# Two row tiles that share each weight chunk, and the exponentials of A's keys one product later

## The chip, the cores and the metric

The kernel runs on one core of a Trainium2 chip. A core has a matrix engine (TensorE, "PE" in the profile), a vector engine (VectorE, DVE), a scalar engine (ScalarE, ACT), GpSimd (POOL) and a queue processor that only issues transfers (SyncE, SP). They run side by side, each through its own list of instructions in order, and wait for each other on semaphores. Matrix products write into PSUM; the other operands lie in SBUF; inputs and outputs lie in HBM and are moved by 16 DMA engines.

The metric is the device time of one execution, in microseconds (us). The kernel before takes 461.2 us, the median of seven runs between 460.77 and 463.86.

## What is computed

x has 2048 rows of 1024 numbers. Two attention blocks read it and a gate per row mixes them:

```python
g = sigmoid((x * gate_w).sum(-1))
a = A(x)          # linear attention: phi(t) = where(t > 0, t + 1, exp(t)) + 1e-6
b = B(x)          # local attention: 8 keys behind each row, 2 apart, softmax
out = g * a + (1 - g) * b
# A: q, k, v = x @ A_wqkv, in 32 heads of 32
#    kv = sum over rows of phi(k)^T v,  z = sum over rows of phi(k)
#    o  = (phi(q) kv) / (phi(q) z),     a = o @ A_wo
# B: q, k, v = x @ B_wqkv, in 32 heads of 32
#    b = (softmax(q k / sqrt(32)) v) @ B_wo
```

The change touches two places: the very first product, x times the v columns of B_wqkv, and the phi of A's keys.

## The kernel before

**Tiles.** The rows of x are taken in 16 tiles of 128. A *pair* is two of them; tile_of(pair, i) names them, so that pair 0 is tiles 0 and 4, pair 1 tiles 1 and 5, pair 2 tiles 2 and 6. xT holds x transposed: the 1024 columns lie as 8 chunks of 128 partitions, so that a product of a tile with 512 columns of weights is eight matmuls (kc 0 to 7) into one PSUM tile. Most products are done as groups with seven products in place of eight, on sums of operands that VectorE makes (class Group, m1 to m7; Weights.sums and xsums make the sums); the sequence of these products is the clock of the program: side() is called after each of them.

**The start.** Before any sum can be there, pairs 0 and 1 are multiplied plainly with the v weights of B (vb_plain, called in L880). The weights arrive in 256 KB pieces: vb_load(k, j) brings the chunks kc = 2k and 2k + 1 of column half j. Piece (0, 0) is issued by ScalarE's queue, all others by SP's. Two tiles, 0 and 4, come as plain rows (xr_load, L189) and are transposed by TensorE (transpose, L469): eight 128x128 transposes into two PSUM tiles, the first half copied to xT by ScalarE, the second by VectorE (L478). All other tiles are transposed by the DMA on the way in (xt_load, L90). SP issues in this order (L191 to L203): rows of tile 0; pieces (1, 0), (2, 0), (3, 0); rows of tile 4; tiles 1 and 5 transposed; the four pieces of half 1; tiles 2, 6, 3 and 7 transposed.

vb_plain first goes through column half 0 tile by tile: tile 0, 4, 1, 5, each with its eight matmuls (L520), then the gate's eight narrow matmuls (gate, L456) and ScalarE's copy out of PSUM (v_final, L244). The transposes of tile 0 stand before kc 0 of tile 0, those of tile 4 before kc 6 of tile 0. Then half 1 is done for all four tiles chunk by chunk. Fourteen matmuls on zeros (warm_up, L467) stand ahead of all this.

**Who sets the order.** TensorE's and SP's lists are as the program writes them (manual_schedule, L40). The lists of the other engines are ordered by a scheduler that keeps to the order of emission, save where high_priority() or issue_after() say otherwise.

**The keys of A.** ka_group multiplies a pair with A's key columns. When the last column half of a tile is in SBUF (tA), done(i) takes a tile eA and calls phi (L543): phi emits the exponential on ScalarE at once, and returns three VectorE steps (maximum, minimum, sum). defer(n, ops) queues such steps; side() adds one to the count of products, state["now"], then calls dve_side(), which emits the next step of the first queue whose time has come, and only then step(), which emits pieces of side work such as the scores of B's attention with their large exponential (PT, L701). qa_group also calls phi, for some of A's queries, and emits all its steps at once.

Of the kernel before, what the change touches and what calls it, by code (L numbers as in the profile page):

```python
# [8 lines left out]
ACT = mybir.ActivationFunctionType  # L9
ALU = mybir.AluOpType  # L10
# [16 lines left out]
def kernel(  # L27
# [11 lines left out]
    nc = tc.nc  # L39
# [13 lines left out]
    def xrows(t):  # L53
        return xpar[t // 8, (t % 8) * P:(t % 8 + 1) * P, :]
# [128 lines left out]
    def vb_load(k, j, q=nc.sync):  # L183
        q.dma_start(out=W[:, 2 * k:2 * k + 2, 512 * j:512 * j + 512],
                    in_=bview[:, 2 * k:2 * k + 2, 2 * D + 512 * j:2 * D + 512 * j + 512])
# [3 lines left out]
    def xr_load(t):  # L189
        xr[t] = ering.tile([P, D], BF16, name="xr", tag="e")  # L190
        nc.sync.dma_start(out=xr[t][:], in_=xrows(t))  # L191
    vb_load(0, 0, nc.scalar)
    xr_load(0)
    vb_load(1, 0)
    vb_load(2, 0)
    vb_load(3, 0)
    xr_load(4)
    for t in (1, 5):
        xt_load(t)
    for k in range(4):  # L200
# [41 lines left out]
    def acc(out_, ps, add):  # L242
        if add is None:
            nc.scalar.copy(out=out_, in_=ps)  # L244
        else:
            last_dve[0] = nc.vector.tensor_tensor(out=out_, in0=ps, in1=add, op=ALU.add).ins
# [3 lines left out]
    class Group:  # L250
# [10 lines left out]
        def mm(self, ps, m, start):  # L261
            for kc in range(self.nk):
                lhsT, rhs = self.operands(m, kc)
                nc.tensor.matmul(ps[:], lhsT=lhsT, rhs=rhs, start=start and kc == 0,  # L264
                                 stop=kc == self.nk - 1, skip_group_check=True)
# [68 lines left out]
    def row_ops(w, pair):  # L334
        p, c = divmod(pair, 4)
        return lambda m, kc: (xop(m, kc, p, slice(c * P, c * P + P)), w.get(m, kc))
# [58 lines left out]
    def defer(products, ops, gap=1):  # L395


        deferred.append([state["now"] + products, list(ops), gap])
# [46 lines left out]
    def tile_of(pair, i):  # L445
        return (pair // 4) * 8 + (pair % 4) + 4 * i
# [5 lines left out]
    def gate(t):  # L452
        p, j = divmod(t, 8)
        hf, c = divmod(j, 4)
        for kc in range(8):
            nc.tensor.matmul(gps[:, t:t + 1], lhsT=xT[p][:, kc, hf, c * P:(c + 1) * P], rhs=gw[:, kc:kc + 1],  # L456
                             start=kc == 0, stop=kc == 7)
# [11 lines left out]
    def transpose(t):  # L469
        p, j = divmod(t, 8)  # L470
        hf, c = divmod(j, 4)
        for k0, tag, copy in ((0, "X1", nc.scalar.copy), (4, "Y1", nc.vector.tensor_copy)):
            tps = ps_pj.tile([P, 512], F32, name="tps", tag=tag)
            tps = tps.bitcast(BF16)[:, 0:512].rearrange("p (k n) -> p k n", k=4)
            for k in range(4):
                nc.tensor.transpose(tps[:, k, :], xr[t][:, (k0 + k) * P:(k0 + k + 1) * P], ident[:])
            with tc.high_priority():
                last_dve[0] = copy(out=xT[p][:, k0:k0 + 4, hf, c * P:(c + 1) * P], in_=tps).ins  # L478


    def v_tiles(name):
        if name == "va":
            return [tring.tile([P, H, 32], BF16, name=name, tag="t") for _ in range(2)]
        vs = [tring.tile([P, H, 33], BF16, name=name, tag="t") for _ in range(2)]
        for v in vs:
            nc.gpsimd.memset(v[:, :, 32:33], 1.0)  # L486
        return vs

    def v_final(vs, by_chunk=False):
        def final(i, j, ps, add):  # L490
            if by_chunk:
                out_ = vs[i][:].rearrange("p (c a h) e -> p a c h e", c=4, a=2)[:, j, :, :, 0:32]
                rs = lambda ap: ap.rearrange("p (c h e) -> p c h e", c=4, e=32)
            else:
                out_ = vs[i][:, 16 * j:16 * j + 16, 0:32]
                rs = lambda ap: ap.rearrange("p (h e) -> p h e", e=32)
            acc(out_, rs(ps), None if add is None else rs(add))
        return final

    def vb_store(vs, pair, i):  # L500
        t = tile_of(pair, i)
        nc.sync.dma_start(out=V_d[t // 8][(t % 8) * P:(t % 8 + 1) * P, :],
                          in_=vs[i][:].rearrange("p h e -> p (h e)"))
# [5 lines left out]
    def vb_plain(*pairs):  # L509


        vs = {pair: v_tiles("va") for pair in pairs}
        tiles = [(pair, i) for pair in pairs for i in range(2)]

        def ps_of(pair, i):
            return ps_pj.tile([P, 512], F32, name="K", tag="XY"[i] + str(pair % 2))

        def mm(ps, pair, i, j, kc):
            p, c = divmod(pair, 4)
            nc.tensor.matmul(ps[:], lhsT=xT[p][:, kc, i, c * P:c * P + P],  # L520
                             rhs=wvB.W[:, kc, 512 * j:512 * j + 512], start=kc == 0, stop=kc == 7,
                             skip_group_check=True)
        for pair, i in tiles:
            ps = ps_of(pair, i)
            for kc in range(8):
                if (pair, i) == tiles[0] and kc in (0, 6):
                    transpose(tile_of(pair, kc // 6))
                mm(ps, pair, i, 0, kc)
            gate(tile_of(pair, i))
            v_final(vs[pair], True)(i, 0, ps[:], None)  # L530
        tiles = tiles[2:] + tiles[:2]
        ps = {t: ps_of(*t) for t in tiles}
        for k in range(4):
            for t in tiles:
                for kc in (2 * k, 2 * k + 1):
                    mm(ps[t], *t, 1, kc)
                if k == 3:
                    pair, i = t
                    v_final(vs[pair], True)(i, 1, ps[t][:], None)
                    vb_store(vs[pair], pair, i)  # L540


    def phi(e, t):  # L543

        nc.scalar.activation(out=e, in_=t, func=ACT.Exp)  # L545
        return [lambda: nc.vector.tensor_scalar(out=t, in0=t, scalar1=0.0, scalar2=None, op0=ALU.max),
                lambda: nc.vector.tensor_scalar(out=e, in0=e, scalar1=1.0, scalar2=EPS, op0=ALU.min, op1=ALU.add),
                lambda: nc.vector.tensor_tensor(out=e, in0=e, in1=t, op=ALU.add)]  # L548

# [3 lines left out]
    def ka_group(w, pair):  # L553
        ts = [tring.tile([P, D], BF16, name="tA", tag="t") for _ in range(2)]

        def final(i, j, ps, add):
            acc(ts[i][:, 512 * j:512 * j + 512], ps, add)

        def done(i):
            e = ering.tile([P, D], BF16, name="eA", tag="e")  # L560
            defer(0, phi(e[:], ts[i][:]))
            pks[tile_of(pair, i)] = e
        return Group(row_ops(w, pair), final, done)

# [70 lines left out]
    def qa_group(w, nn, p):  # L635
        ts = [tring.tile([P, 2, 512], BF16, name="tq", tag="t") for _ in range(2)]
        es = [ering.tile([P, 2, 512], BF16, name="eq", tag="e") for _ in range(2)]
        out = qa_out(es, nn, p)

        def final(i, j, ps, add):  # L640
            acc(ts[i][:, j, :], ps, add)

        def done(i):
            for f in phi(es[i][:], ts[i][:]):
                f()
            add_side(8, out(i), p, "oa")
        return Group(col_ops(w, p), final, done)
# [228 lines left out]
    def gates(*pairs):  # L876
        for pair in pairs:
            for i in range(2):
                gate(tile_of(pair, i))
    vb_plain(0, 1)  # L880
    x_loads(4, 5)
    ws, xs = wvB.sums(), xsums(2)
# [117 lines left out]
```

## Time and profile before

| what | us |
|---|---|
| median of seven runs | 461.2 |
| the profiled execution | 460.77 |
| its span, first to last instruction | 459.0 |
| TensorE busy | 443.2 |
| VectorE busy | 283.1 |
| ScalarE busy | 236.9 |
| GpSimd busy | 59.7 |
| 16 exponentials eA of 1024 columns, each | 1.06 |
| 16 large exponentials PT, each | 1.87 |
| 512-column matmul L520, mean of one in the records | 0.38 |

The page is one execution. A record of a matmul is longer than its slot, since matmuls are pipelined: in a run of them the starts stand 0.22 us apart. Where the page says "x<-y", x is written and y is read; "<-DMA xr" behind a row in brackets says for whom the engine stood idle, and how long. The 40 digits of the page's second part are slices of 11.5 us each:

```profile
PE   7999999998999999999999999999999999999996
...
DMA  9799911690301703007030056291229772795111
```

The reader is to see that in the first slice TensorE is busy to seven tenths only, while the DMA engines are nearly full.

### The profile page before, as it was taken

To read this page: it belongs to the slowest core of one execution; us is meant where nothing else is said; L and a number is where in the kernel's file an instruction comes from. 1 tells how busy PE (TensorE), PEld (TensorE's weight loads), DVE (VectorE), ACT (ScalarE), POOL (GpSimd) and SP (SyncE) were. 2 spreads that over 40 slices of the span, in tenths; PEclk is the share of its full clock that TensorE was granted. 3 is DMA by queue.
4 is the path that set the end of the run, shared out by engine and by line. 5 is a ranking of instruction groups with operands and counts; after the bars stand their busy time and mean duration, and the time that the engine had idled before them with its cause. 6 is when DMAs were issued, how large, how long until landed. Compare 5 with 4: busy or idle time off the path is not lost.

```text
span 459.0 us, 11712 instructions
## 1 busy us (share of the span) xinstructions
PE 443.2 (97%) x5017; PEld 216.4 (47%) x5070; DVE 283.1 (62%) x452; ACT 236.9 (52%) x345; POOL 59.7 (13%) x119
## 2 busy tenths in 40 slices
PE   7999999998999999999999999999999999999996
PEld 4455444444444444444445444445554444444444
DVE  0456768669748387485774846769777973256112
ACT  2234357567476484673855847536677544222221
POOL 8000000000000000000000000007686313000000
PEclk9999999999999999999999999999999999999999
DMA  9799911690301703007030056291229772795111
GB/s 213 155 231 225 306 26 70 200 197 3 99 4 36 157 1 101 1 26 164 6 99 2 26 131 193 90 263 47 71 72 222 169 169 91 148 212 134 48 46 46
DMA packets 111956, 51.62 MB, mean 112 GB/s; under 512 B 75552, under 2 KB 107552, under 8 KB 111904
## 3 DMA queue, kind: packets, MB, share of 16 engines
q1 hardware_dynamic: 111600, 50.61, 45.5%
q8 instruction: 39, 0.64, 0.6%
q10 hardware_dynamic: 272, 0.26, 0.2%
q14 instruction: 13, 0.11, 0.1%
q0 software_dynamic: 32, 0.00, 0.0%
HBM read 26.22 MB, written 16.78 MB: 94 GB/s over the span
## 4 chain that ended last, share of the span: by engine, by line
PE 89%; ACT 6%; DMA 1%; issue 1%; DVE 0%; SPq 0%; ACTq 0%; DVEq 0%
PE X L264 41%; PE Y L264 28%; PE Q L661 9%; PE K L520 3%; ACT PT L701 3%; PE o L712 2%; PE oA L618 2%; ACT eA L545 2%; PE s L696 1%; DMA xr<-in_A_x_dram 1%; PE kps L579 1%; ACT tA L244 1%; PE o L717 1%; PE Y L299 1%; ACT U2s L273 1%
## 5 line engine op out<-in xcount | busy, mean ns | idle before, releaser
L264 PEld LDWEIGHTS <-xT 128*128 128x128 bf16 (+1 forms) x352 | 33.0, 98 | 39.7 <-issue 1.8
L264 PE MATMUL X<-T,SS 128*128 128x512 f16 x176 | 45.3, 380 | 0.7 <-ACT U2s L273 0.7
L264 PEld LDWEIGHTS <-WS 128*128 128x128 bf16 (+1 forms) x288 | 28.1, 98 | 33.6
L661 PE MATMUL Q<-xT,WS 128*128 128x512 bf16 x186 | 43.1, 379 | 0.3
L264 PE MATMUL X<-SS,TS 128*128 128x512 f16 x144 | 37.0, 379 | 3.9 <-ACT U2s L273 3.9
L273 ACT COPY U4s<-X 128x512 f32<-128x512 f32 x40 | 23.4, 584 | 33.0 <-PE X L264 32.9
L486 POOL MEMSET vA<- 128x32 bf16 x16 | 4.0, 250 | 269.6 <-DVE eA L548 144.8
L264 PE MATMUL Y<-W,xT 128*128 128x512 bf16 (+1 forms) x151 | 38.8, 379 | 0.0
L264 PEld LDWEIGHTS <-SS 128*128 128x128 f16 x264 | 24.2, 98 | 29.7 <-issue 2.8
L701 ACT ACTIVATE PT<-s 128x2048 bf16<-128x2048 f32 x16 | 29.9, 1869 | 15.1 <-PE s L696 15.0
L264 PE MATMUL Y<-xT,WS 128*128 128x512 bf16 (+1 forms) x144 | 36.9, 379 | 0.0
L264 PEld LDWEIGHTS <-TS 128*128 128x128 f16 x216 | 20.4, 97 | 29.0 <-issue 5.9
L702 DVE TENSOR_TENSOR PT<-PT,maskp 128x2048 bf16<-128x2048 bf16 x16 | 19.6, 1224 | 22.1 <-ACT PT L701 22.1
L273 ACT COPY M1s<-X 128x512 f32<-128x512 f32 x40 | 23.6, 589 | 11.5 <-PE X L264 10.4
L661 PEld LDWEIGHTS <-WS 128*128 128x128 bf16 x192 | 18.3, 98 | 20.1
L273 ACT COPY U2s<-X 128x512 f32<-128x512 f32 x40 | 23.3, 583 | 8.2 <-PE X L264 8.2
L264 PEld LDWEIGHTS <-oT 128*128 128x128 bf16 (+1 forms) x176 | 17.2, 98 | 20.5
L629 POOL TENSOR_TENSOR obA<-ofv,rec 128x512 bf16<-128x512 f32 x22 | 25.7, 1187 | 0.9
L724 DVE COPY nB<-o 128x1024 f32<-128x1024 f32 x16 | 19.6, 1222 | 6.0 <-ACT rB L723 6.0
L723 ACT ACTIVATE rB<-o 128x1024 f32<-128x1024 f32 x16 | 16.4, 1023 | 12.3 <-DVE oB L730 9.5
L264 PE MATMUL X<-T,oS 128*128 128x512 f16 x96 | 22.7, 379 | 0.0
L264 PE MATMUL X<-W,SS 128*128 128x512 bf16 x86 | 22.5, 379 | 0.1
(140 smaller groups left out, 760.2 us busy)
## 6 DMA issues: line engine op xcount, KB each, us to landing
V_d<-va SPq DMA_DIRECT2D x16, 256.0 KB, 3.2
WS<-in_B_wqkv_dram SPq DMA_DIRECT2D x16, 256.0 KB, 4.5
W<-in_A_wqkv_dram SPq DMA_DIRECT2D x8, 512.0 KB, 6.2
vw<-V_d SPq DMA_DIRECT2D x16, 256.0 KB, 4.3
OB_d<-oB SPq DMA_DIRECT2D x16, 256.0 KB, 2.2
OA_d<-obA SPq DMA_DIRECT2D x16, 256.0 KB, 2.3
out_dram<-osb SPq DMA_DIRECT2D x30, 128.0 KB, 1.8
oT<-OB_d SPq DMA_DIRECT2D x12, 256.0 KB, 4.0
```

The source lines that it names most:

```text
L264: nc.tensor.matmul(ps[:], lhsT=lhsT, rhs=rhs, start=start and kc == 0, stop=kc == self.nk - 1, skip_group_check=True)
L273: nc.scalar.copy(out=s[:], in_=ps[:])
L520: nc.tensor.matmul(ps[:], lhsT=xT[p][:, kc, i, c * P:c * P + P], rhs=wvB.W[:, kc, 512 * j:512 * j + 512], start=kc == 0, stop=kc == 7, ski ...
L545: nc.scalar.activation(out=e, in_=t, func=ACT.Exp)
L618: nc.tensor.matmul(o[:, k, 132 * j:132 * j + 132], lhsT=es[i][:, j, k * P:(k + 1) * P], rhs=KVz[:, nn + 4 * j, :], start=True, stop=True)
L629: nc.gpsimd.tensor_tensor(out=ob[:, k:k + 2], in0=of[:, k:k + 2, :, 0:32], in1=rec[:, k:k + 2].broadcast_to([P, 2, 8, 32]), op=ALU.mult)
L661: nc.tensor.matmul(ps[:], lhsT=w.W[:, kc, j * P:j * P + P], rhs=xT[p][:, kc, i, :], start=kc == 0, stop=kc == 7, skip_group_check=True)
L701: nc.scalar.activation(out=PT[:], in_=s[:], func=ACT.Exp, scale=SCALE)
L702: nc.vector.tensor_tensor(out=PT[:], in0=PT[:], in1=maskp[:, None, :].broadcast_to([P, 4, 512]), op=ALU.mult)
L712: nc.tensor.matmul(o[32 * g:32 * g + 32, 2 * b, cols], lhsT=vw[rows, j, 4 * ch + g, :], rhs=PT[rows, g, cols], start=True, stop=True)
L723: nc.scalar.activation(out=rB[:], in_=o[:, 1:4:2, :], func=ACT.Ln)
L724: nc.vector.tensor_copy(out=nB[:], in_=o[:, 0:4:2, :])
```

## The change

There are three edits.

- SP issues the rows of tile 4 directly behind the rows of tile 0, ahead of the three weight pieces.
- vb_plain takes tiles 0 and 4 through half 0 together, two chunks at a time: kc 0 and 1 of tile 0, then of tile 4, then kc 2 and 3 of tile 0, and so on. The transposes of each stand before its own kc 0. Their gates and copies out of PSUM follow behind both. Tiles 1 and 5 are done as before.
- phi no longer emits the exponential itself: the exponential becomes part of its first deferred step, together with the maximum. ka_group defers by 1 in place of 0. qa_group calls all steps at once, as before.

```diff
--- before.py
+++ after.py
@@ -191,10 +191,10 @@
         nc.sync.dma_start(out=xr[t][:], in_=xrows(t))
     vb_load(0, 0, nc.scalar)
     xr_load(0)
+    xr_load(4)
     vb_load(1, 0)
     vb_load(2, 0)
     vb_load(3, 0)
-    xr_load(4)
     for t in (1, 5):
         xt_load(t)
     for k in range(4):
@@ -520,14 +520,20 @@
             nc.tensor.matmul(ps[:], lhsT=xT[p][:, kc, i, c * P:c * P + P],
                              rhs=wvB.W[:, kc, 512 * j:512 * j + 512], start=kc == 0, stop=kc == 7,
                              skip_group_check=True)
-        for pair, i in tiles:
-            ps = ps_of(pair, i)
-            for kc in range(8):
-                if (pair, i) == tiles[0] and kc in (0, 6):
-                    transpose(tile_of(pair, kc // 6))
-                mm(ps, pair, i, 0, kc)
-            gate(tile_of(pair, i))
-            v_final(vs[pair], True)(i, 0, ps[:], None)
+        ps = {t: ps_of(*t) for t in tiles[:2]}
+        for k in range(4):
+            for t in tiles[:2]:
+                if k == 0:
+                    transpose(tile_of(*t))
+                for kc in (2 * k, 2 * k + 1):
+                    mm(ps[t], *t, 0, kc)
+        for t in tiles:
+            if t not in ps:
+                ps[t] = ps_of(*t)
+                for kc in range(8):
+                    mm(ps[t], *t, 0, kc)
+            gate(tile_of(*t))
+            v_final(vs[t[0]], True)(t[1], 0, ps[t][:], None)
         tiles = tiles[2:] + tiles[:2]
         ps = {t: ps_of(*t) for t in tiles}
         for k in range(4):
@@ -542,8 +548,8 @@
 
     def phi(e, t):
 
-        nc.scalar.activation(out=e, in_=t, func=ACT.Exp)
-        return [lambda: nc.vector.tensor_scalar(out=t, in0=t, scalar1=0.0, scalar2=None, op0=ALU.max),
+        return [lambda: (nc.scalar.activation(out=e, in_=t, func=ACT.Exp),
+                         nc.vector.tensor_scalar(out=t, in0=t, scalar1=0.0, scalar2=None, op0=ALU.max)),
                 lambda: nc.vector.tensor_scalar(out=e, in0=e, scalar1=1.0, scalar2=EPS, op0=ALU.min, op1=ALU.add),
                 lambda: nc.vector.tensor_tensor(out=e, in0=e, in1=t, op=ALU.add)]
 
@@ -558,7 +564,7 @@
 
         def done(i):
             e = ering.tile([P, D], BF16, name="eA", tag="e")
-            defer(0, phi(e[:], ts[i][:]))
+            defer(1, phi(e[:], ts[i][:]))
             pks[tile_of(pair, i)] = e
         return Group(row_ops(w, pair), final, done)
```

## The prediction

> **What bounds the kernel now.** I read the page's busy times first, then the chain of waits over the first 60 us, then the timeline from 0 to 40 us and the landing times of single DMA issues, and last the order of the instructions of both built programs on each engine. The busy times say that TensorE sets the time: no other engine is near it.
>
> ```profile
> PE 443.2 (97%) x5017; PEld 216.4 (47%) x5070; DVE 283.1 (62%) x452; ACT 236.9 (52%) x345; POOL 59.7 (13%) x119
> ```
>
> So only a place where TensorE stands still, or an instruction taken from it, can move the end. The change takes no TensorE instruction away. The chain of waits (start, length, what) shows one long step that isn't TensorE's, right at the start:
>
> ```profile
> 2.67 6.24 DMA xr<-in_A_x_dram
> 8.96 0.62 PE tps L476 x8
> 9.58 0.43 PE K L520 x2
> ...
> 11.94 0.18 PE gps L456 x8
> 12.12 1.75 PE K L520 x8
> ```
>
> The second row load is issued at 2.67, lands 6.24 later, and only then can TensorE transpose tile 4. A whole product of a tile costs 1.75, or 0.216 for one of eight matmuls, and a gate 0.18. The timeline of the same stretch (start, length, engine, line, what):
>
> ```profile
> 0.74 0.39 SPq L191 DMA_DIRECT2D xr<-in_A_x_dram  x1
> 1.20 1.43 SPq L184 DMA_DIRECT2D W<-in_B_wqkv_dram  x3
> 2.67 0.47 SPq L191 DMA_DIRECT2D xr<-in_A_x_dram  x1
> ...
> 4.52 1.04 PE L476 MATMUL tps<-ident,xr 128*128 128x128 bf16 x8 [0.16 <-POOL maskp L217]
> 5.17 0.58 ACT L478 COPY xT<-tps 128x512 bf16<-128x512 bf16 x1 [3.15 <-PE tps L476]
> 5.81 1.89 PE L520 MATMUL K<-W,xT 128*128 128x512 bf16 x6 [0.25 <-ACT xT L478]
> ...
> 8.96 0.62 PE L476 MATMUL tps<-ident,xr 128*128 128x128 bf16 x8 [1.26 <-DMA xr<-in_A_x_dram]
> ...
> 9.39 0.58 ACT L478 COPY xT<-tps 128x512 bf16<-128x512 bf16 x1 [3.64 <-PE tps L476]
> ...
> 11.98 1.89 PE L520 MATMUL K<-W,xT 128*128 128x512 bf16 x8
> ```
>
> The reader is to see three things. TensorE idles 1.26 (1.42 by issue slots: the sixth matmul starts at 7.32 and needs 0.22) before the second eight transposes. The first product of tile 1 starts at 11.98; everything up to there belongs to tiles 0 and 4. And all five loads before 3.19 stand in one line on SP's queue.
>
> **The change, part one: the start.** SP's issue of the tile 4 rows moves ahead of three weight loads. Landings, each issue's start plus its latency in the trace: first rows 0.74 + 3.7 = 4.5; chunk 0 (ACT's queue) 0.77 + 4.4 = 5.2; chunks 1, 2, 3 at 1.20 + 4.7 = 5.9, 1.66 + 5.4 = 7.1, 2.16 + 6.1 = 8.2; tile 4 rows 2.67 + 6.2 = 8.9. Consecutive landings are 0.7 to 1.2 apart and all six loads are 256 KB, so I treat the landings as slots in order of issue. Tile 4's rows then take the slot at 5.9 (no later than 7.1, if the fabric serves them one slot late); chunks 1, 2, 3 land at 7.1, 8.2 and 8.9. The sum of bytes is unchanged, so the transposing loads of tiles 1 and 5 behind them, which land at 3.19 + 6.6 = 9.8 and 5.03 + 6.3 = 11.3, stay there.
>
> TensorE's new order, from the same start 5.81: two matmuls of tile 0, at 5.81 and 6.21; their weight loads stand 0.4 apart and the third comes at 6.53. The eight transposes of tile 4 therefore begin at 6.53, with their rows there since 5.9. The first half of the tile is copied by ScalarE: in the trace that copy starts 0.43 after the transposes (9.39 against 8.96), takes 0.58, and a matmul follows 0.05 behind the copy in the first tile (5.17 + 0.58 to 5.81). So tile 4's first matmul starts at 6.53 + 0.43 + 0.58 + 0.06 = 7.60. Transposes end near 7.0, so TensorE now idles about 0.6 for the copy, which before was hidden behind tile 0's last two matmuls and its gate. Then 14 matmuls follow: 14 x 0.216 = 3.02, to 10.62. Chunks are needed at 7.60 + 0.43 = 8.03, 8.89 and 9.76, against landings at 7.1, 8.2 and 8.9: 0.7 to 0.9 to spare each. Two gates at 0.2 each (9.85 to 10.05 in the trace) bring tile 1's first product to **11.03 instead of 11.98: 0.95 less**. Its columns landed at 9.8; tile 5 is needed at 12.96 and landed at 11.3. With the rows a slot late (7.1) the same sum gives 11.6, a gain of 0.4; with no wait for the copy at all it would be 1.55, which nothing here allows.
>
> What is late next? The second halves of the weights land by 14.8 and are first used at 14.9. VectorE's sums for pair 2 hang on a transposing load, not on TensorE:
>
> ```profile
> 18.26 0.42 DVE L100 TENSOR_TENSOR SS<-xT 128x512 f16<-128x512 bf16 x1 [4.13 <-DMA xT<-in_A_x_dram]
> ...
> 22.35 0.42 DVE L102 TENSOR_TENSOR SS<-xT,SS 128x512 f16<-128x512 bf16 x1
> ...
> 23.42 0.43 DVE L103 TENSOR_TENSOR xT<-xT 128x512 f16<-128x512 bf16 x1 [0.65 <-PE gps L456]
> ...
> 26.33 1.03 PE L264 MATMUL Y<-T3v,xT 128*128 128x512 f16 x4
> ```
>
> These sums stay at 18.26 to 22.77; the last one (L103) waits for TensorE's gates and moves up to 22.77, ending at 23.2, while its matmul comes at 25.4 instead of 26.33. There are 2.2 to spare. From the V_d stores at 22.45 on, SP's loads follow TensorE's results, with DMA idle from 20 to 22, so they move up too. I find nothing tied to absolute time behind that, and let the 0.95 run through to the end.
>
> **A rule against it.** "TensorE: Matmul & The Clock Gate", section "HAM oscillation — how this bites in real kernels", says to run all chunks of one tile before waiting for DMA, since an idle window of about 3.4 us drops the clock to half; the change does the opposite. Taken by its letter, 14 matmuls at the 0.4 of the first two cost 14 x 0.2 = 2.8 more, and the sum is 1.9 slower. The row: after 1.26 idle before tile 4's transposes the eight took 0.62 against 1.04 for tile 0's, and the matmuls behind them stand 0.216 apart. (The granted clock reads 1.00 in both stretches; only the spacing shows the slow beginning.) The longest stretch without products is 6.53 to 7.60 in the new order, shorter than the old 7.54 to 9.42, so I take the row.
>
> **Part two: the exponentials.** They matter for TensorE where one stands before a large exponential on ScalarE:
>
> ```profile
> 104.02 1.06 ACT L545 ACTIVATE eA<-tA 128x1024 bf16<-128x1024 bf16 x1
> ...
> 104.99 1.86 ACT L701 ACTIVATE PT<-s 128x2048 bf16<-128x2048 f32 x1
> ...
> 106.74 0.58 ACT L273 COPY U2s<-X 128x512 f32<-128x512 f32 x1
> ...
> 107.37 0.81 PE L264 MATMUL X<-SS,TS 128*128 128x512 f16 x3 [0.61 <-ACT U2s L273]
> ```
>
> The view of waits has 4.5 us of this kind in 7 stalls. But the edit can't reach them: side() raises the product count before it looks at deferred work, so an entry of delay 1 comes out in the same call as one of delay 0, and dve_side() runs ahead of the step() that emits the large exponential. The built programs agree: on ScalarE, VectorE and GpSimd the order is the same throughout, and every wait after the start is on the same count; TensorE differs in its first 160 instructions alone, SP in four issues. Cost and gain: nothing.
>
> **Sum.** Span 459.0 - 0.95 = 458.05; the profiled execution took 460.77, 1.77 more than its span, so 459.8. The median of the seven runs is 461.2: **460.3**.
>
> **Rivals.**
> - Nothing arrives (0.12): the lead is eaten by a later load. Against it are the margins above; for it, only that the first 20 us are DMA-bound. 461.2.
> - The rows land a slot late (0.12): gain 0.4, 460.8. For it: packets of ACT's queue share the engines.
> - More than the sum (0.10): without the profiler the old wait for the rows is longer than 1.26, by 0.5 or so; gain 1.5, 459.7. Nothing in this profile shows it.
> - Slower (0.06): the clock falls back in the pause near 7.0. It decides from the moment that the 14 matmuls start 0.3 apart: 0.95 / 14 = 0.07 over the 0.216 is break-even; at 0.4 it is 461.2 + 1.9 = 463.1.
> - That the exponentials do move is worth up to -4.5 (455.8); the instruction order excludes it.
>
> The forecast has 0.60.
>
> **Numbers.** Change from no change can be told at about 0.3%, or 1.4 us; 0.95 lies inside it. Six of the seven runs lie within 1.0 us and one is 2.7 above, so a median may be off by 0.4; of the forecast's 0.60 I put 0.20 beyond the bound. Faster: 0.20 + 0.10 = 0.30. Slower: 0.06. Within: 0.40 + 0.12 + 0.12 = 0.64. Range: a gain of 1.5 less 0.3 of scatter below gives 459.4; no gain plus 0.2 above, 461.4.
>
> **What would show it.** In the new profile: tile 4's transposes at 6.5, not 8.96; an idle time of 0.6 before its first product, put down to ScalarE's copy; tile 1's first product near 11.0; V_d's first store near 21.5; the seven stalls on U2s unchanged at 0.6 each. A DMA wait in place of the copy's would say that the slots are wrong; tile 1 at 11.0 with an unchanged span, that a later wait ate it; matmuls 0.4 apart after 7.6, that the clock rule holds.

## The result, and the profile after

The changed kernel takes 459.69 us (median of 17 runs, 458.92 to 460.14) against 461.11 us for the kernel before (40 runs, 460.51 to 464.04). The ratio is 0.9963, with a 95% interval of 0.9953 to 0.9973: **1.4 us faster**. That lies just beyond the bound of 0.3%, and the interval reaches over it. The forecast was 460.3, inside the bound. One more execution of the changed kernel, of 461.21, stands in the record outside these 17; with it the median would be 459.75. The two profiled executions took 460.77 and 459.5, with spans of 459.0 and 457.7.

The busy times of the page after answer to the line shown of before:

```profile
PE 442.4 (97%) x5017; PEld 216.4 (47%) x5070; DVE 283.2 (62%) x452; ACT 236.8 (52%) x345; POOL 59.7 (13%) x119
```

The counts are the same, so no work went. In the chain of waits over the first 60 us, the DMA step of 6.24 us is gone, and two of ScalarE's copies stand there instead (start, length, what):

```profile
4.37 0.42 PE tps L476 x4
4.81 0.59 ACT xT L478
5.45 0.60 PE K L520 x2
6.06 0.24 PE tps L476 x4
6.32 0.59 ACT xT L478
6.96 3.20 PE K L520 x14
10.15 0.38 PE gps L456 x16
```

The timeline of the changed kernel from 0 to 40 us (start, length, engine, line, what, and in brackets the idle time before):

```profile
0.74 0.87 SPq L191 DMA_DIRECT2D xr<-in_A_x_dram  x2
...
1.66 1.45 SPq L184 DMA_DIRECT2D W<-in_B_wqkv_dram  x3
...
4.24 0.76 PE L476 MATMUL tps<-ident,xr 128*128 128x128 bf16 x8
...
5.45 0.60 PE L520 MATMUL K<-W,xT 128*128 128x512 bf16 x2 [0.45 <-ACT xT L478]
...
5.89 0.61 PE L476 MATMUL tps<-ident,xr 128*128 128x128 bf16 x8
...
6.96 3.20 PE L520 MATMUL K<-W,xT 128*128 128x512 bf16 x14 [0.45 <-ACT xT L478]
...
10.39 1.89 PE L520 MATMUL K<-W,xT 128*128 128x512 bf16 x7
...
21.83 0.42 DVE L103 TENSOR_TENSOR xT<-xT 128x512 f16<-128x512 bf16 x1
...
24.74 1.03 PE L264 MATMUL Y<-T3v,xT 128*128 128x512 f16 x4
```

Both row loads are issued first, tile 4's transposes run at 5.89 instead of 8.96, and tile 1's first product starts at 10.39 instead of 11.98: **1.59 earlier, where 0.95 was forecast**. From there TensorE and what follows it move as one block: ScalarE's copies are 1.58 to 1.59 earlier at 20 us, at 100 and at 280. VectorE's sums for pair 2, which wait for a load, begin 0.98 earlier (17.28 instead of 18.26). Two small losses follow. A wait of the products o that the profile gives no cause for is 0.60 in this execution and 0.46 in the other, at about 289, and the output products wait 0.23 for a load (oT from OA_d) at 347. The span keeps 1.3.

The exponentials stand where they stood, in the changed kernel's timeline near 102 us:

```profile
102.44 1.06 ACT L551 ACTIVATE eA<-tA 128x1024 bf16<-128x1024 bf16 x1
...
103.40 1.86 ACT L707 ACTIVATE PT<-s 128x2048 bf16<-128x2048 f32 x1
...
105.16 0.58 ACT L273 COPY U2s<-X 128x512 f32<-128x512 f32 x1
105.78 1.02 PE L264 MATMUL X<-SS,TS 128*128 128x512 f16 x4 [0.61 <-ACT U2s L273]
```

This is the order and the stall of 0.61 of before, all 1.58 to 1.59 earlier.

### The profile page after: what moved, and what is told of

It reads as the page before. It is cut to its first block, busy times and chain, and to the rows that moved or that the text cites. A ratio compares the mean times of both kernels' runs of the same rounds, so it can differ in the third digit from the quotient of the medians.

```text
span 457.7 us, 11713 instructions
## 1 busy us (share of the span) xinstructions
PE 442.4 (97%) x5017; PEld 216.4 (47%) x5070; DVE 283.2 (62%) x452; ACT 236.8 (52%) x345; POOL 59.7 (13%) x119
## 4 chain that ended last, share of the span: by engine, by line
PE 91%; ACT 7%; issue 1%; DVE 0%; ACTq 0%; DVEq 0%
PE X L264 41%; PE Y L264 28%; PE Q L667 9%; PE K L520 3%; ACT PT L707 3%; PE o L718 2%; PE oA L624 2%; ACT eA L551 2%; PE s L702 1%; PE kps L585 1%; ACT tA L244 1%; PE o L723 1%; PE Y L299 1%; ACT U2s L273 1%; PE gps L467 1%
```

## The experiments

All ratios are to the kernel before, measured on the same chip beside it.

**1. Each edit by itself.** Four kernels.

The first edit alone:

```diff
     xr_load(0)
+    xr_load(4)
     vb_load(1, 0)
     vb_load(2, 0)
     vb_load(3, 0)
-    xr_load(4)
```

> The kernel before with the first edit alone: rows of tile 4 issued second, products tile by tile as before. Theory (the gain is the idle time before tile 4's transposes, and the weight chunks take the late slots): the rows are no longer waited for, but chunks 2 and 3 land at about 8 and 8.8, and tile 0 needs them first; tile 1's first product comes 2.6 behind chunk 3, near 11.3 instead of 11.98: 0.5 to 0.8 faster, ratio 0.9985. Rival (the rows' place alone makes the gain): tile 1 near 10.4, ratio 0.9963. Rival (it needs both): no gain.

Measured: 460.75, ratio 0.9997 (0.9985 to 1.0008). No gain that can be seen. TensorE's timeline in its one profile:

```profile
5.57 1.04 PE L520 MATMUL K<-W,xT 128*128 128x512 bf16 x2 [0.25 <-ACT xT L478]
6.96 2.08 PE L520 MATMUL K<-W,xT 128*128 128x512 bf16 x4 [0.35 <-DMA W<-in_B_wqkv_dram]
8.83 1.06 PE L476 MATMUL tps<-ident,xr 128*128 128x128 bf16 x8
...
12.59 1.89 PE L520 MATMUL K<-W,xT 128*128 128x512 bf16 x8
```

Tile 1's first product is at 12.59, and the products stand 0.43 apart until about 10: in the trace's record the clock first rises to full at 10.37.

The second edit alone is the interleaved loop of vb_plain as in the change, with SP's order as before.

> The kernel before with the second edit alone: tiles 0 and 4 share each chunk, but the rows of tile 4 are still issued behind the weights. Theory: transposes of tile 4 at 8.9 as before, then copy 1.06, 14 products 3.02 and two gates 0.4, so tile 1's first product at 13.4: 1.4 slower, ratio 1.003. Rival (sharing a chunk helps by itself): not slower than before.

Measured: 464.71, ratio 1.0072 (1.0058 to 1.0086). Slower, and by 3.7 instead of 1.4. TensorE's timeline in its profile:

```profile
5.47 1.03 PE L520 MATMUL K<-W,xT 128*128 128x512 bf16 x2 [0.25 <-ACT xT L478]
9.89 1.03 PE L476 MATMUL tps<-ident,xr 128*128 128x128 bf16 x8 [3.39 <-DMA xr<-in_A_x_dram]
11.18 4.61 PE L520 MATMUL K<-W,xT 128*128 128x512 bf16 x14 [0.25 <-ACT xT L478]
```

The rows of tile 4 landed 0.9 later than in the first profile of before, and TensorE ran at half speed on both sides of an idle time of 3.39: the first two products stand 0.43 apart, and the 14 behind the wait took 4.61, where the changed kernel needs 3.20. In the trace's record the clock first rises at 14.07, so this wait shows no fall of it; the clock was not up yet. (In four of the six executions the mean granted clock is 0.996, as one fall would make it.) Tile 1's first product came at 16.02. So the sum of this expectation had the right steps (13.4), and misses 0.9 of landing, 1.4 of slow products and 0.2 of slow transposes.

The third edit alone:

```diff
-        nc.scalar.activation(out=e, in_=t, func=ACT.Exp)
-        return [lambda: nc.vector.tensor_scalar(out=t, in0=t, ...),
+        return [lambda: (nc.scalar.activation(out=e, in_=t, func=ACT.Exp),
+                         nc.vector.tensor_scalar(out=t, in0=t, ...)),
...
-            defer(0, phi(e[:], ts[i][:]))
+            defer(1, phi(e[:], ts[i][:]))
```

> The kernel before with the third edit alone. Theory: the instructions of every engine stand in the same order, so nothing: ratio 1.000, the seven stalls on U2s of 0.6 stay. Rival: the exponentials give the missing 0.5 us, ratio 0.999, and some of the seven stalls are gone. Its profile is also a second look at the start of the kernel before: by the theory that the old wait swallows whatever comes early, tile 1's first product stays near 11.9 even where the clock rises or the first rows land earlier.

Measured: 461.10, ratio 1.0007 (0.9990 to 1.0024); the seven stalls are all there. The edit does nothing, which also makes this kernel a second sample of the kernel before. Its profiled execution happens to be its longest one, 463.71, and shows what a long execution of the old start is made of. TensorE's timeline:

```profile
5.32 1.04 PE L520 MATMUL K<-W,xT 128*128 128x512 bf16 x4 [0.45 <-ACT xT L478]
6.95 0.59 PE L520 MATMUL K<-W,xT 128*128 128x512 bf16 x2 [0.59 <-DMA W<-in_B_wqkv_dram]
9.90 0.62 PE L476 MATMUL tps<-ident,xr 128*128 128x128 bf16 x8 [2.36 <-DMA xr<-in_A_x_dram]
10.36 0.59 PE L520 MATMUL K<-W,xT 128*128 128x512 bf16 x2
...
11.00 3.46 PE L520 MATMUL K<-W,xT 128*128 128x512 bf16 x8
14.25 0.40 PE L456 MATMUL gps<-gw,xT 128*128 128x1 bf16 x8
14.51 1.90 PE L520 MATMUL K<-W,xT 128*128 128x512 bf16 x8
```

The first product starts at 5.32, half a microsecond earlier than in the first profile of before, and it helps nothing: the rows land at 2.68 + 7.2 = 9.9, TensorE waits 2.36, and the clock, which had risen at 4.32, falls to half from 11.14 to 14.56, for tile 4's products (3.46 instead of 1.89).

The first two edits together, without the third:

> The changed kernel without its third edit. Theory: all of the change, ratio 0.9963. Rival: 0.5 us less gain, ratio 0.9974. Its profile is a second look at the changed start: the time of tile 1's first product varies with the first landing and with the moment at which the clock rises (10.4 in the first look, 11.0 forecast from the slower start of before).

Measured: 459.41, ratio 0.9959 (0.9946 to 0.9972): the whole change. Its first product starts at 5.47, tile 1 at 10.41. The first edit alone gives nothing, the second alone costs 3.7, and together they give 1.6: neither can be read without the other.

**2. The clock, the copy and the exponentials.** Four kernels. The first puts the exponentials where the words of the change say:

```diff
+        def exp():
+            with tc.issue_after(last_act[0]):
+                nc.scalar.activation(out=e, in_=t, func=ACT.Exp)
-        return [lambda: (nc.scalar.activation(out=e, in_=t, func=ACT.Exp),
-                         nc.vector.tensor_scalar(out=t, ...)),
+        return [lambda: (exp(), nc.vector.tensor_scalar(out=t, ...)),
...
-            defer(1, phi(e[:], ts[i][:]))
+            defer(2, phi(e[:], ts[i][:]))
```

(last_act[0] is set to each copy that save() makes.)

> The changed kernel with its exponentials really moved: two products behind the row's end, and tied behind the last U copy on ScalarE, so that they stand behind the large exponential PT. Theory (the third edit moves nothing, but the stalls come from that order): PT starts 1.06 earlier, the seven stalls of 0.6 on U2s go, 4 us and more faster than the changed kernel: 455, ratio to before 0.987. Rival (the exponential then stands before another copy, or holds VectorE's maximum before an eviction): the stalls come back elsewhere, ratio near 0.996 as for the changed kernel, or above.

Measured: 456.04, ratio 0.9892 (0.9870 to 0.9913). By the two ratios to before this is 3.3 faster than the changed kernel, as are the spans of the two profiles, 454.4 and 457.7. TensorE's waits over the whole execution (who, for whom: us in total, times, longest), first of the changed kernel, then of this one:

```profile
PE X L264 <- ACT U2s L273: 4.5, 7, 0.7
...
PE o L718 <- issue: 0.6, 1, 0.6
PE o L718 <- DVE nB L730: 0.6, 1, 0.6
```

```profile
PE o L721 <- DVE nB L733: 2.1, 5, 1.0
...
PE o L721 <- issue: 1.0, 1, 1.0
```

All seven stalls on U2s are gone. Some of it comes back: the products o wait 2.1 instead of 0.6 for nB, VectorE's copy out of PSUM. Four of the five waits, 0.24 to 0.36 each, stand where an exponential now runs directly ahead of rB (ScalarE's read of the same product), which nB follows. The fifth and largest does not:

```profile
109.52 1.22 DVE L733 COPY nB<-o 128x1024 f32<-128x1024 f32 x1
109.53 1.05 ACT L554 ACTIVATE eA<-tA 128x1024 bf16<-128x1024 bf16 x1
...
110.79 0.74 PE L721 MATMUL o<-PT,vw 64*32 64x57 bf16 x72 [1.02 <-DVE nB L733]
```

The exponential runs beside this copy, and VectorE's sums stand before it, as in the changed kernel. There the same wait is 0.58; TensorE now comes to it earlier. Theory and rival both hold a part.

In the second, tile 0's second chunk is multiplied while tile 4's transposes are copied:

```diff
                     transpose(tile_of(*t))
+                    if t == tiles[1]:
+                        for kc in (2, 3):
+                            mm(ps[tiles[0]], *tiles[0], 0, kc)
+                if k == 1 and t == tiles[0]:
+                    continue
```

> The changed kernel with tile 0's second chunk multiplied while tile 4's transposes are copied. Theory (the copy's 0.45 idle is on the path, chunk 1 lands at 6.6): 0.1 to 0.35 faster than the changed kernel, tile 1's first product at 10.1 to 10.3 instead of 10.4; ratio to before 0.9955. Rival (the weight chunks would then be waited for): tile 1 at 10.4 or later, ratio 0.996 or above.

Measured: 459.72, ratio 0.9967 (0.9954 to 0.9980). In its profile the copy is no longer waited for behind tile 4's transposes, and tile 1's first product is at 10.30, though the first two products stood 0.38 apart at the slow clock and the transposes began at 6.23. The expected gain is smaller than what the intervals can tell, so this one decides nothing: no gain is seen in the medians.

In the third, 12 matmuls on zeros fill the old wait for tile 4's rows:

```diff
                 if (pair, i) == tiles[0] and kc in (0, 6):
+                    if kc:
+                        warm_up(12)
                     transpose(tile_of(pair, kc // 6))
```

> The kernel before with 12 matmuls on zeros (1.3 us at full clock) put into the wait for tile 4's rows. They do no work, they only keep TensorE busy. Theory (in a share of executions of the kernel before the clock falls in the wait, as the second look at it showed: 8 products in 3.46 instead of 1.89 behind a wait of 2.4): the median falls by 0.3 to 1, ratio 0.998 or 0.999, and the spread shrinks. Rival (the clock has no part in the typical run; rows landing later than in the first look make the difference): ratio 1.000 to 1.002, spread unchanged.

Measured: 461.29, ratio 1.0001 (0.9991 to 1.0012). The median doesn't move, so the rival is right for the usual execution: the clock has no part in it. The long executions may be another matter: none of the 11 runs is above 462.03, while 4 of the 12 runs of the third edit alone, which has the old order, lie between 462.88 and 463.71. But the kernel before had only one in 25 above 462.1 beside it, so that the filling removes them isn't shown by these runs alone. Its profile has the rows at about 9.0 and tile 1 at 12.09; the matmuls on zeros ran until 9.08, about 0.1 past the landing.

In the fourth, the changed kernel has one warm-up matmul in place of 14 (warm_up(1)).

> The changed kernel with one warm-up matmul in place of 14. Theory (its start hangs on the clock, not on a landing): first two products, transposes and some of the 14 run at half speed until about 9.5, tile 1 at 11.4 to 12, so 1 to 1.6 slower than the changed kernel and near the kernel before: ratio 0.999. Rival (the start hangs on landings): ratio 0.996.

Measured: 461.17, ratio 0.9996 (0.9984 to 1.0007). The gain is gone:

```profile
7.52 5.07 PE L520 MATMUL K<-W,xT 128*128 128x512 bf16 x14 [0.25 <-ACT xT L478]
...
12.83 1.89 PE L520 MATMUL K<-W,xT 128*128 128x512 bf16 x8
```

Its 14 products take 5.07 instead of 3.20, and tile 1 comes at 12.83, later still than expected; the clock first rises at 11.35. The new start hangs on TensorE and its clock, and no longer on a landing.

**3. What stayed open.** Four more kernels. The first edit alone once more, with matmuls on zeros in its waits:

```diff
+                if (pair, i) == tiles[0] and kc in (2, 4):
+                    warm_up(4)
                 mm(ps, pair, i, 0, kc)
```

> The run with the first edit alone, with eight matmuls on zeros more: four ahead of tile 0's chunk 1 and four ahead of its chunk 2. They do no work, they fill the waits for chunks. Theory (the first edit alone gained nothing because its short waits kept the clock at half: its first look shows 0.43 per product until about 10): tile 1's first product at 11.3, ratio to before 0.9985. Rival (it is the chunks that tile 0 waits for, in their late slots): ratio 0.999 to 1.000, tile 1 near 12.

Measured: 460.98, ratio 0.9985 (0.9967 to 1.0003): not told from nothing by its interval. Its profile tells more, with the products at full speed throughout:

```profile
6.37 0.59 PE L520 MATMUL K<-W,xT 128*128 128x512 bf16 x2
...
8.23 0.59 PE L520 MATMUL K<-W,xT 128*128 128x512 bf16 x2 [0.83 <-DMA W<-in_B_wqkv_dram]
8.66 0.61 PE L476 MATMUL tps<-ident,xr 128*128 128x128 bf16 x8
9.10 0.59 PE L520 MATMUL K<-W,xT 128*128 128x512 bf16 x2
```

Chunk 2 has taken a late slot and lands at 8.2; tile 0 waits for it, and transposes, two products, a gate and the eight products of tile 4 still follow: tile 1 comes at 11.66. The expectation reckoned 2.6 from chunk 3; what counts is chunk 2, and the 3.4 behind it hold two products and the transposes more. So the first edit alone only puts a wait for a chunk in place of the wait for the rows. That the clock came up late besides (10.37) was seen in one profile, and the medians with and without the filling, 460.75 and 460.98, show no gain from mending it.

The kernel before once more, one profile:

> The kernel before once more, one look. Theory (the old start ends at the landing of tile 4's rows plus 3.07, whenever the first rows land): tile 1's first product 3.0 to 3.1 behind that landing, or later if the clock falls. Rival (it hangs on the first rows): it moves with their landing.

Measured: 461.24 in one run. TensorE's timeline:

```profile
5.29 1.04 PE L520 MATMUL K<-W,xT 128*128 128x512 bf16 x4 [0.46 <-ACT xT L478]
...
8.73 0.62 PE L476 MATMUL tps<-ident,xr 128*128 128x128 bf16 x8 [1.18 <-DMA xr<-in_A_x_dram]
...
11.75 1.46 PE L520 MATMUL K<-W,xT 128*128 128x512 bf16 x6
```

The first product is at 5.29 instead of 5.81, and tile 1 at 11.75: it follows the rows, which landed at 2.68 + 6.0 = 8.7, by 3.07.

The moved exponentials on the old start:

> The kernel before with the exponentials moved behind PT as in the run on the changed kernel, and without the two edits of the start. Theory (start and exponentials add up): 3.6 faster than before, 457.5, ratio 0.992. Rival (the one needs the other): 0.995 or above.

Measured: 458.12, ratio 0.9940 (0.9917 to 0.9962). The product with the change's 0.9963 is 0.990, and both together measured 0.9892: within the intervals they add up. Its profile has the rows at 8.9 and tile 1 at 11.98.

And the changed kernel with the exponentials behind PT and the maximum one product behind them:

```diff
-        return [lambda: (exp(), nc.vector.tensor_scalar(out=t, ...)),
+        return [exp, lambda: nc.vector.tensor_scalar(out=t, ...),
```

> The changed kernel with the exponentials behind PT, and VectorE's maximum one product behind the exponential instead of beside it, so that the second exponential of a pair stands behind the copies out of PSUM on ScalarE. Theory (the 2.1 us of new waits of the products o on the copies nB and rB come from exponentials that stand before those copies): up to 1 faster than the run with the maximum beside it, ratio to before 0.987 to 0.989. Rival (the waits come from the copies' own length): same, 0.989.

Measured: 455.24, ratio 0.9871 (0.9850 to 0.9892). TensorE's waits:

```profile
PE o L721 <- issue: 1.6, 1, 1.6
...
PE o L721 <- DVE nB L733: 1.0, 1, 1.0
```

Of the five waits for nB the four behind an exponential are gone, and the largest is left. The wait put down to "issue" grew from 1.0 to 1.6. Its median is 0.8 below that of the run with the maximum beside the exponential; the two intervals overlap. This is the fastest version here: 5.9 us below the kernel before measured beside it, and by the ratios 4.2 below the changed kernel.

## Why the prediction was right, and where its size was off

- **The mechanism.** Right. The wait for tile 4's rows was on the path, went, and little behind the start ate of the lead: 1.59 at tile 1, 1.3 in the span, 1.4 in the medians. The range held, but the median lies only 0.3 above its lower end, and the gain is half as large again as the 0.95 of the sum.
- **The slots.** Right. Landings in the changed kernel are 5.6 for the rows of tile 4 and 6.6, 7.8, 8.6 for chunks 1 to 3, against 5.9 and 7.1, 8.2, 8.9 forecast, and no product waits for a chunk. One reading was off without harm: VectorE's sums for pair 2 did not stay at 18.26 but began at 17.28, since their load landed earlier too. At their old time they would still have been done about 1.5 before their matmul at 24.74.
- **The copy.** Right: from tile 4's transposes to its first product 6.96 - 5.89 = 1.07, as forecast, and 3.43 from there to tile 1, against 3.02 + 0.41 = 3.43.
- **The term that was off** is "from the same start 5.81", with the first two matmuls 0.40 and 0.32 apart. I carried both from one execution of the old kernel into the new order. The changed kernel's first product started at 5.45, and its first two products took 0.44 to the transposes instead of 0.72: 0.36 + 0.28 = 0.64, which is the whole difference between 0.95 and 1.59. That the prediction named 1.55 as the gain with no wait for the copy is a coincidence: the copy is waited for, 0.45.
- **Why that term is treacherous.** In the old order it didn't count. In three profiles with these products at full clock, the start of before itself among them, tile 1 came 3.07 behind the landing of tile 4's rows (8.91, 8.68, 8.91), while the first product started at 5.81, 5.29 and 5.53. In the new order tile 1 follows the first product: by 4.94 in the first three profiles that have the new start as it is (5.45, 5.47, 5.56), and by 5.16 in the fourth (5.23). The profile of before was a poor place to read the first product's time from, because nothing there depended on it. The clock is a part of it: it first rises at 6.40 in the profile of before and at 4.57 in that of the changed kernel, but elsewhere at 4.04 to 7.08 with the old start and at 4.16 to 6.16 with the new and its 14 warm-up matmuls, so this goes with the execution and not with the order. What makes the first rows land at 4.5 in two profiles of the old load order and between 3.8 and 4.2 in all others, of both orders, wasn't tried.
- **The clock rule.** The row was rightly preferred for the change: behind the pauses of 0.45 the products ran at full speed. But the rule wasn't idle. It hit the old order, in the one long execution that was profiled (wait of 2.36), so the prediction feared it on the wrong side.
- **A second gain, which the medians don't show.** The record gives each execution's mean granted clock. One fall to half for 3.41 us, as in the profiled long execution, makes 1 - 1.71 / 460 = 0.996. Of the 71 executions of the kernel before beside the experiments, 9 read 0.995 or 0.996, and they took 462.2 to 463.8; of the 39 with the new start and all 14 warm-up matmuls, none is below 0.998. Nor is any of the 23 with a filled wait (wait_warm and sp_warm). This speaks for the old wait as the cause of most long executions; the fall itself was seen in one trace only.
- **The exponentials.** Nothing, as forecast, and the seven stalls stood. What moved them were a delay of 2 and a tie to a later instruction together; which of the two did it isn't shown, since no run has one without the other. The 4.5 us of stalls were about the right price: 3.1 to 4.2 came when they went.
- **The rivals.** "More than the sum" named the size, 1.5, with the wrong cause (a longer old wait); the new start was faster instead. Rows a slot late, and a lead that is eaten, did not come.

## What to carry to other kernels

Where a change removes the wait that a stretch ends with, times inside that stretch that nothing depended on come onto the path; take them from several executions, or carry a range for them, before building the new order on one. Two edits that only work together have to be reckoned together: here the load order alone gives nothing and the loop order alone is 3.7 us slower. Where a scheduler orders an engine, look at the built order before crediting a move in the source, and if the stall that the move was for is real, tie the instruction down and measure that. Look at the spread as well as the median: a wait that is gone can also take rare long executions with it.

## What was not expected of the hardware

- In the 14 traces all 16 whole stretches between two changes of the clock on record are multiples of 3.413 us. In the long execution the clock rose at 4.32, fell at 11.14, two such steps later, and rose again at 14.56. The step that ended in the fall, 7.73 to 11.14, held 2.2 of idle time, then eight transposes, two products and a gate. In the first profile of before the step from 6.40 to 9.81 held 1.4 of idle time, and the clock stayed. The Trainium skill, "TensorE: Matmul & The Clock Gate", section "The HAM clock gate (the "warmup" mystery)", speaks of an idle window of about 3.4; this drop came at the end of a step that was idle for about two thirds only.
- The granted clock of a stretch has to be read with care at the start of a kernel. For the execution of the third edit alone, its windows (busy time of TensorE, weight load, VectorE, ScalarE and GpSimd, then granted clock, DMA share, GB/s) read 0.52 where the products are 0.43 apart:

```profile
11.00:14.50 3.50, 3.50 (x22) 1.41 (x19) 0.57 (x1) 0.58 (x2) 1.55 (x9) 0.52 0.97 286
```

For the second edit alone, in a stretch with the same spacing of 0.43, it reads 1.00:

```profile
11.00:14.00 3.00, 2.82 (x7) 1.04 (x8) 0.59 (x2) 0.12 (x1) 1.55 (x9) 1.00 0.99 291
```

The clock record of each trace begins with the first rise, here at 14.07, and what lies ahead of it is counted as full. So a slow start reads 1.00 too, and only the spacing of the products shows it.

- The same six loads in the same order ended between 8.7 and 9.9 in six profiles of the old load order. In the changed order the last of them landed at 8.6 to 8.9. Why wasn't tried.
